# Attention followed by expert routing on one core: expert work set between attention steps, domain ids loaded in runs, transposes set between output tiles

## The chip, the cores and the metric

The kernel runs on one core of a Trainium2 chip. The metric is device time in microseconds (us); what is compared is the median of several executions. Engines: TensorE (PE; PEld is its weight load), VectorE (DVE), ScalarE (ACT), GpSimd (POOL) and SyncE (SP). DMAs are issued from SP, ACT and POOL, each in the order of its own instruction stream.

## What is computed

```python
q_pool = q.reshape(B, H, S // 2, 2, D).mean(axis=3)      # B = 8, H = 8, S = 1152, D = 64
scores = scale * np.matmul(q_pool, k.transpose(0, 1, 3, 2))
attn = np.exp(scores - max) / sum
x = np.matmul(attn, v)                                   # as (B * 576, 512): 4608 tokens
for e in range(8):
    mask = domain_id == e
    out[mask] = np.maximum(x[mask] @ w1[e], 0.0) @ w2[e] # 512 -> 1024 -> 512
```

Queries are pooled in pairs, attention runs over all 1152 keys, and each of the 4608 tokens then goes through the one expert that its domain id names. The ids do not depend on the attention.

## The kernel before

**Attention.** The 64 heads are taken as 32 pairs, four pairs to a batch. A pair is 12 steps, 384 steps `t` in all (`p`, `s_` are the pair and the step in it). In a step TensorE makes the scores of 432 query-key columns for both heads (`score`, L410; two PSUM buffers `s`), ScalarE takes the exponential of them in one instruction (`expo`, L425), and in nine of twelve steps TensorE also multiplies one earlier block of exponentials with the values (`av`, L435: ten matmuls of 65 columns). The table `AVS` (L477) says in which steps: all but 2, 6 and 10 of a pair, the last two falling into the next pair. `evac` (L449) divides by the sums and writes the pair's part of `xb`, the batch's rows, with VectorE. Loads run ahead by two or three pairs: queries on SyncE (`load_q`, three buffers), keys and values on POOL (`load_k`, `load_v`, three buffers each). `prep_q`, `prep_k`, `prep_v` cast and sort them on VectorE, and `burst_k`, `burst_q` transpose them on TensorE in steps 2 and 6 for the next pair, by one of two PSUM buffers `tp`.

**Routing.** `rt_a` to `rt_d` and `rt_tok` work out on VectorE, with two small matmuls (L199, L204), to which row of the DRAM tensor `x_slot` each token goes: 640 slots an expert, of which the first 256 are kept for tokens of the first four batches (`KO`, `IB`), and an overflow area. The ids come by nine small copies on ScalarE's queue (L158). `init_x` fills the 640-slot areas with a pattern in four copies on SyncE; it depends on `pat` alone. After the last pair of a batch, `put_x` scatters its rows to `x_slot` from POOL (`scatter`, L338). Weights of experts 0 to 4 are loaded by POOL from step 60 on.

**Experts.** After the attention the pools of the attention are released, and `run` (L621) takes one expert at a time: `get_x` loads its slots, `turn` transposes them (per tile of 128 slots four matmuls and one copy by VectorE or ScalarE), `stage1` and `stage2` are the two matrix products, and each tile of output rows is scattered to `out` by POOL. Experts 0 to 2 run in two parts, first their 256 early slots, then the other 384; experts 3 to 7 run with all 640 at once.

**What sets the order.** Each engine executes in the order in which the program is written (`manual_schedule`); what waits for what is worked out by a tracker of tiles and of whole DRAM tensors. Two writes into `x_slot`, or a read and a write, wait for each other in program order, except scatters among themselves, which are declared free of each other (group `xscat`).

## Time and profile before

| | us |
|---|---|
| runs | 538.62, 539.15, 542.89; median 539.15 |
| the profiled execution | 537.33 |
| its span, first to last instruction | 535.5 |
| PE, ACT, DVE, POOL busy in it | 462.0, 351.0, 220.3, 163.5 |
| mean granted TensorE clock | 0.948 |

The page of the profile gives busy times, the span in 40 slices, the DMA queues, the chain of work that ended last, and groups of instructions by line. Its other views list instructions in order of time (start, length, engine, line, what is written <- what is read, how many, and in brackets the idle time before and what ended it), the waits summed by who waited for whom, stretches of time with each engine's busy time, and DMA issues with their median time to landing. A busy TensorE is not TensorE at its peak, since the ends of matmuls are modelled; their starts are not.

### The profile page before, as it was taken

Reading aid. Unit: us, or ns where it says so; the run is one execution under the profiler, and the core shown is the slowest. Engines: PE = TensorE matmul, PEld = TensorE weight load, DVE = VectorE, ACT = ScalarE, POOL = GpSimd, SP = SyncE. Lnnn points to the kernel's source line nnn. Section 1 sums busy time; section 2 is a strip of 40 time slices with the busy share of each in tenths; the row PEclk is TensorE's granted clock in tenths of the full one; section 3 lists DMA queues with packets and bytes.
Section 4 is the critical chain, followed back from the end, with each engine's and each line's share of the span. In section 5 each row is a group of like instructions: output and inputs, shape, how many; then the busy total and the mean of one; then the engine's idle time right before and its main releaser. Section 6 shows DMA issues by size and latency. Waiting matters only on the chain.

```text
span 535.5 us, 12899 instructions
## 1 busy us (share of the span) xinstructions
PE 462.0 (86%) x5536; PEld 323.6 (60%) x5536; DVE 220.3 (41%) x515; ACT 351.0 (66%) x470; POOL 163.5 (31%) x278
## 2 busy tenths in 40 slices
PE   6038999999999999999999999539899999999990
PEld 3026777777777777777777777425544555455440
DVE  4038545455554555545455553102332223223220
ACT  1117999999999999999999999512222323223310
POOL 5001108207225145154173040111335521321321
PEclk9558999999999999999999999959999999999996
DMA  9969846988999949959969930022329994221211
GB/s 227 224 125 241 199 92 143 245 171 173 237 184 193 215 106 223 190 114 231 215 127 236 195 69 2 15 91 69 109 78 220 238 248 149 96 95 44 85 61 37
DMA packets 57172, 80.48 MB, mean 150 GB/s; under 512 B 8590, under 2 KB 43150, under 8 KB 57104
## 3 DMA queue, kind: packets, MB, share of 16 engines
q0 software_dynamic: 34928, 49.54, 47.4%
q1 hardware_dynamic: 17424, 29.99, 19.9%
q10 hardware_dynamic: 4752, 0.02, 0.8%
q8 instruction: 45, 0.74, 0.6%
q14 instruction: 23, 0.19, 0.1%
HBM read 95.46 MB, written 20.49 MB: 217 GB/s over the span
## 4 chain that ended last, share of the span: by engine, by line
ACT 47%; issue 26%; DMA 11%; POOL 8%; DVE 2%; PE 2%; POOLq 0%; ACTq 0%; SPq 0%; DVEq 0%
ACT e L431 47%; POOL out_dram L341 6%; DMA w2h<-in_moe_w_dram 5%; DMA dom<-in_moe_domain_id_dram 3%; DMA x_slot<-pat 2%; PE s L419 1%; POOL x_slot L341 1%; PE acc L442 1%; POOL gap L339 1%; DMA xs<-x_slot 1%; DMA x_slot<-xb,addr 0%; DVE xb L459 0%; DVE sc L212 0%; POOLq L341 0%; POOL vs L96 0%
## 5 line engine op out<-in xcount | busy, mean ns | idle before, releaser
L431 ACT ACTIVATE e<-s 128x864 f16<-128x864 f32 x384 | 302.1, 899 | 38.2 <-DMA dom<-in_moe_domain_id_dram 23.1
L419 PE MATMUL s<-qz,kq 128*128 128x432 f16 (+2 forms) x1152 | 205.9, 287 | 23.4 <-ACT e L431 22.4
L442 PEld LDWEIGHTS <-e 128*128 128x128 f16 x2880 | 127.8, 98 | 41.7 <-DVE xb L459 2.8
L442 PE MATMUL acc<-v,e 128*128 128x65 f16 x2880 | 136.6, 194 | 2.4 <-DVE xb L459 2.1
L419 PEld LDWEIGHTS <-kq 128*128 128x128 f16 x1152 | 102.2, 97 | 49.7 <-issue 30.3
L341 POOL DMA_INDIRECT x_slot<-xb,addr x40 | 43.5, 1087 | 130.0 <-issue 130.0
L591 PE MATMUL hp<-xt,w1h 128*128 128x128 f16 (+3 forms) x512 | 75.9, 301 | 5.0 <-DVE xt L579 3.2
L341 POOL DMA_INDIRECT out_dram<-osb,xs x40 | 39.6, 990 | 121.3 <-ACT osb L613 101.9
L607 PE MATMUL op<-w2h,hT 128*128 128x512 f16 x320 | 70.9, 379 | 0.0
L591 PEld LDWEIGHTS <-w1h 128*128 128x128 f16 x512 | 43.8, 98 | 36.6 <-issue 8.1
L596 ACT ACTIVATE hT<-hp 128x640 f16<-128x640 f32 (+2 forms) x44 | 24.6, 559 | 51.1 <-PE hp L591 48.8
L613 ACT COPY osb<-op 128x512 f32<-128x512 f32 x24 | 14.1, 586 | 60.0 <-PE op L607 60.0
L457 DVE RECIPROCAL rr<-acc 128x5 f32<-128x5 f32 x64 | 12.2, 190 | 100.0 <-PE acc L442 100.0
L607 PEld LDWEIGHTS <-hT 128*128 128x128 f16 x320 | 31.1, 98 | 35.6
L598 DVE TENSOR_SCALAR hT<-hp 128x640 f16<-128x640 f32 (+2 forms) x44 | 28.3, 643 | 55.0 <-PE hp L591 53.8
L96 POOL DMA_DIRECT2D vs<-in_v_dram x32 | 23.8, 743 | 79.5 <-DVE v L366 77.7
L459 DVE TENSOR_TENSOR xb<-acc,rr 128x320 f16<-128x320 f32 x64 | 31.5, 492 | 2.8 <-DVE rr L457 0.4
L357 DVE TENSOR_TENSOR qp<-q 96x768 f16<-96x768 f32 x32 | 30.2, 945 | 1.5 <-DMA q<-in_q_dram 1.5
L615 DVE COPY osb<-op 128x512 f32<-128x512 f32 x16 | 11.1, 692 | 45.5 <-PE op L607 45.5
L404 DVE COPY qz<-tp 64x576 f16<-64x576 f16 x64 | 28.7, 449 | 1.0
L575 PE MATMUL xp<-ident,xs 128*128 128x128 f16 x160 | 14.0, 223 | 16.7 <-DMA xs<-x_slot 13.1
L375 DVE COPY kp<-k 128x576 f16<-128x576 f16 x62 | 25.0, 445 | 2.6 <-DMA k<-in_k_dram 2.6
(80 smaller groups left out, 232.3 us busy)
## 6 DMA issues: line engine op xcount, KB each, us to landing
q<-in_q_dram SPq DMA_DIRECT2D x32, 576.0 KB, 7.4
vs<-in_v_dram POOLq DMA_DIRECT2D x32, 288.0 KB, 10.1
k<-in_k_dram POOLq DMA_DIRECT2D x31, 288.0 KB, 10.6
w1h<-in_moe_w_dram POOLq DMA_DIRECT2D x16, 512.0 KB, 8.4
w2h<-in_moe_w_dram POOLq DMA_DIRECT2D x16, 512.0 KB, 14.8
x_slot<-pat SPq DMA_DIRECT2D x4, 1285.0 KB, 11.6
xs<-x_slot SPq DMA_DIRECT2D x5, 642.5 KB, 9.5
xs<-x_slot SPq DMA_DIRECT2D x3, 385.5 KB, 3.1
```

Of the source, the lines that this page charges most:

```text
L341: ins = nc.gpsimd.indirect_dma_start(out=dst[:, :], out_offset=bass.IndirectOffsetOnAxis(ap=ap, axis=0), in_=src, in_offset=None, **kw,)
L357: nc.vector.tensor_tensor(out=qp[:, :, :, :].rearrange("p j h d -> p h j d"), in0=q2[:, :, :, 0:D], in1=q2[:, :, :, D : 2 * D], op=ALU.add,)
L375: nc.vector.tensor_copy(kp[:, :, hh, :], loaded[p]["k16"][:, hh, :, :])
L404: nc.vector.tensor_copy(qz[p % 2][r][lo : lo + 64, :], mt[lo : lo + 64, P : P + Sp])
L419: nc.tensor.matmul(s[:, r, o : o + n], lhsT=kq[p][:, c * P : (c + 1) * P], rhs=qz[p % 2][r][:, q0 : q0 + n], start=True, stop=True,)
L431: nc.scalar.activation(e_[:, :, o : o + W], st.pop(t)[:, :, 0:W], AF.Exp, bias=0.0, scale=0.0625)
L442: nc.tensor.matmul(acc[p][h][:, i * (D + 1) : (i + 1) * (D + 1)], lhsT=e_[:, h, o + QO[i] : o + QO[i] + P], rhs=v16[p % NV][:, c, h, 0 : D ...
L459: nc.vector.tensor_tensor(out=xb[b][:, :, hh * D : (hh + 1) * D], in0=a[:, :, 0:D], in1=rr[:, :].unsqueeze(2).broadcast_to([P, NQ, D]), op ...
L591: nc.tensor.matmul(hp_[:, lo : lo + n], lhsT=w1h[:, cc, f * P : (f + 1) * P], rhs=xt[:, cc, lo : lo + n], start=cc == 0, stop=cc == ND - 1,)
L596: nc.scalar.activation(hT[:, f, 0:m], hp_[:, 0:m], AF.Relu)
L598: nc.vector.tensor_scalar(out=hT[:, f, 0:m], in0=hp_[:, 0:m], scalar1=0.0, scalar2=None, op0=ALU.max)
L607: nc.tensor.matmul(op_[:, :], lhsT=hT[:, f, i * P : (i + 1) * P], rhs=w2h[:, f, :], start=f == 0, stop=f == NF - 1,)
```

## The change

Five things are changed together.

1. The ids are loaded by one copy on SyncE as they lie, 96 partitions with 12 words in a run for each of eight batches, and VectorE copies them to their places in steps 14 to 19 (`rt_dom`). Query pair 1 is loaded from ScalarE's queue, which also casts half of the first keys. The first value and key loads of POOL stand behind its set-up.
2. Routing runs in steps 14 to 33 instead of up to step 15, `init_x` in steps 34, 37, 40 and 43 instead of 20 to 29. In steps 36 to 43, eight new scatters, one per expert, write pattern rows behind each expert's overflow rows; the list of overflowed tokens that was made at the end goes away (`g_over`; this branch runs only when an expert has over 640 tokens).
3. Experts 0 to 3 have their first 256 slots computed in the attention's steps. Each is cut into 17 units: one of transposes, eight of the first product, eight of the second. From step 220 on one unit stands at the end of steps 0, 4, 7 and 10 of a pair. They share one PSUM buffer (`mpsum`), for which `tpsum` goes from two to one. What is left when the steps end runs straight behind them.
4. Behind the attention come one part of 256 slots (expert 4), five of 384 (experts 0 to 4) and three of 640 (5 to 7). Loads are issued two parts ahead, and the transposes of the next part stand between the output tiles of the present one.
5. The ids' copy into `xb` by POOL stands after the last pair of a batch instead of before the first.

**SyncE, from the third load to query pair 6.** Before (`q_232`, `q_439`, `q_646`, `q_843`, `q_1038` are query pairs 2 to 6; brackets name the semaphores waited for, DMASW of POOL's DMAs, DMAHW of the other queues'):

```order
L87 DMA q_232<-in_q_dram 96x2x768
L87 DMA q_439<-in_q_dram 96x2x768 [waits DMAHW6_49,DMAHW2_49,DVE_49]
L166 DMA x_slot<-pat 128x10x514 [waits DMAHW7_49,Pool_49]
L166 DMA x_slot<-pat 128x10x514 [waits DMAHW0_49]
L87 DMA q_646<-in_q_dram 96x2x768 [waits DMAHW3_49,DMAHW1_49,DVE_49]
L166 DMA x_slot<-pat 128x10x514 [waits DMAHW2_49]
L166 DMA x_slot<-pat 128x10x514 [waits DMAHW3_49]
L87 DMA q_843<-in_q_dram 96x2x768 [waits DMAHW4_49,DVE_49]
L644 TENSOR_LOAD ovi [waits DVE_49]
```

Now (`q_211` to `q_858` are pairs 2 to 5, `q_1072` is pair 6):

```order
L119 DMA dom<-in_moe_domain_id_dram 96x8x12
L88 DMA q_211<-in_q_dram 96x2x768
L88 DMA q_387<-in_q_dram 96x2x768 [waits DMAHW2_49,DVE_49]
L88 DMA q_623<-in_q_dram 96x2x768 [waits DMAHW3_49,DVE_49]
L165 DMA x_slot<-pat 128x10x514 [waits DMAHW0_49,Pool_49]
L88 DMA q_858<-in_q_dram 96x2x768 [waits DMAHW5_49,DMAHW1_49,DVE_49]
L741 TENSOR_LOAD ovi [waits DVE_49]
L741 ISA x2
L165 DMA x_slot<-pat 128x10x514 [waits DMASW3_49]
L165 DMA x_slot<-pat 128x10x514 [waits DMASW7_49,DMASW6_49,DMASW4_49]
L165 DMA x_slot<-pat 128x10x514 [waits DMASW3_49,DMAHW4_49,DMASW1_49,DMASW0_49]
L88 DMA q_1072<-in_q_dram 96x2x768 [waits DMAHW6_49,DVE_49]
```

The last three initialising copies now wait for DMAs of POOL (the scatters between them in the program), and query pair 6 stands behind all four instead of query pair 5.

**POOL, steps 40 to 50 of the change** (`vs` is value pair 6, `k_1112` key pair 7; DMAHW3 and DMAHW4 are the third and fourth initialising copy):

```order
L349 DMA x_slot<-pat,padr 41984x514 [waits DMAHW3_49,DMASW0_49]
L347 MEMSET gap 1x1 [waits Pool_49]
L349 DMA x_slot<-pat,padr 41984x514 [waits DMASW1_49]
L97 DMA vs<-in_v_dram 128x2x576 [waits DMASW2_49,DVE_49]
L347 MEMSET gap 1x1 [waits Pool_49]
L349 DMA x_slot<-pat,padr 41984x514 [waits DMASW3_49]
L347 MEMSET gap 1x1 [waits Pool_49]
L349 DMA x_slot<-pat,padr 41984x514 [waits DMAHW4_49,DMASW4_49]
L471 COPY xb<-tok 128x5 [waits DVE_49]
L105 DMA k_1112<-in_k_dram 128x2x576 [waits DMASW5_49,DVE_49]
```

Before, only loads stood here ahead of the first `put_x`; now scatters that wait for the initialising copies stand ahead of these loads.

**TensorE, the end of a step with a unit** (`acc` is a value product, `m` a unit of the second product, `s` the next step's scores):

```order
L450 LDWEIGHTS e
L450 MATMUL acc_4382<-v_0_97,e 128x65
L547 LDWEIGHTS h_4023
L547 MATMUL m<-w2h,h_4023 128x512
L547 LDWEIGHTS h_4023
L547 MATMUL m<-w2h,h_4023 128x512
L427 LDWEIGHTS kq
L427 MATMUL s<-qz_0_93,kq 128x432
```

Before, the scores of the next step stood right behind the value products.

The diff, cut to what the steps above speak of:

```diff
+    mpsum = att.enter_context(tc.tile_pool(name="mpsum", bufs=1, space=bass.MemoryType.PSUM))
-    tpsum = att.enter_context(tc.tile_pool(name="tpsum", bufs=2, space=bass.MemoryType.PSUM))
+    tpsum = att.enter_context(tc.tile_pool(name="tpsum", bufs=1, space=bass.MemoryType.PSUM))
...
     load_q(0)
-    load_v(0)
-    load_k(1)
-    load_v(1)
-    load_q(1)
+    dom = perm.tile([QP, B, NJ, 2], I32, name="dom")
+    nc.sync.dma_start(
+        dom[:, :, :, :].rearrange("p b j t -> p b (j t)"),
+        moe_domain_id.bitcast(I32).rearrange("(b p j t) -> p b (j t)", b=B, p=QP, j=NJ),
+    )
...
-    for i in range(NQ):
-        m, end = 0, 64 if i == 0 else P
-        while m < end:
-            j, pp = divmod(QO[i] + m, QP)
-            n = min(QP - pp, end - m)
-            nc.scalar.dma_start(dom[m : m + n, :, i : i + 1], dv_[pp : pp + n, :, j, 0:1])
-            m += n
...
+    load_v(0)
+    load_k(1)
+    load_v(1)
...
+    def rt_dom(j):
+        if j == 0:
+            nc.vector.memset(dal[64:P, :, 0:1], -1.0)
+        for a in range(QP // 32):
+            x = j * QP + 32 * a
+            i, m = (0, x) if x < 64 else (1 + (x - 64) // P, (x - 64) % P)
+            nc.vector.tensor_copy(dal[m : m + 32, :, i], dom[32 * a : 32 * a + 32, :, j, 0])
...
+        nc.vector.tensor_tensor(out=padr[:, :], in0=ov[:, :], in1=padb[:, :], op=ALU.add)
...
+    load_q(1, nc.scalar)
...
+    def add_expert(e):
+        h0 = {}
+
+        def u_load():
+            h0["xs"] = get_x(fill, e, 0, NA)
+
+        def u_turn():
+            mt = mpsum.tile([P, NA, ND, P], F16, name="m")
+            for i in range(NA):
+                for cc in range(ND):
+                    nc.tensor.transpose(
+                        mt[:, i, cc, :], in_=h0["xs"][:, i, cc * P : (cc + 1) * P],
+                        identity=ident16[:, :],
+                    )
+            h0["xt"] = fill.tile([P, ND, NA * P], F16, name="xt0")
+            nc.vector.tensor_copy(
+                h0["xt"][:, :, :].rearrange("p c (i n) -> p i c n", i=NA), mt[:, :, :, :]
+            )
+
+        def u_up(f):
+            if f == 0:
+                h0["h"] = fill.tile([P, NF, NA * P], F16, name="h0")
+            mt = mpsum.tile([P, 512], FP32, name="m")
+            for cc in range(ND):
+                nc.tensor.matmul(
+                    mt[:, 0 : NA * P], lhsT=wts[e][0][:, cc, f * P : (f + 1) * P],
+                    rhs=h0["xt"][:, cc, :], start=cc == 0, stop=cc == ND - 1,
+                )
+            nc.vector.tensor_scalar(
+                out=h0["h"][:, f, :], in0=mt[:, 0 : NA * P], scalar1=0.0, scalar2=None, op0=ALU.max
+            )
+
+        def u_down(i, g):
+            if g == 0:
+                h0["o"] = mpsum.tile([P, 512], FP32, name="m")
+            for f in (2 * g, 2 * g + 1):
+                nc.tensor.matmul(
+                    h0["o"][:, :], lhsT=h0["h"][:, f, i * P : (i + 1) * P], rhs=wts[e][1][:, f, :],
+                    start=f == 0, stop=f == NF - 1,
+                )
+            if 2 * g + 2 == NF:
+                osb = fill.tile([P, Dm], FP32, name="osb0")
+                nc.vector.tensor_copy(osb[:, :], h0["o"][:, :])
+                scatter(out, osb[:, :], h0["xs"][:, i, Dm:XW].bitcast(I32), "oscat", N - 1)
...
-        if t in (20, 23, 26, 29):
-            init_x((t - 20) // 3)
+        if t in (34, 37, 40, 43):
+            init_x((t - 34) // 3)
+        if 36 <= t < 36 + E:
+            scatter(x_dram, pat[:, :], padr[:, t - 36 : t - 35], "xscat")
...
+        if t == 212:
+            for e in range(FE):
+                add_expert(e)
+            loads.pop(0)()
+        if t >= 220 and main and s_ in FS and units:
+            units.pop(0)()
...
+    while units:
+        units.pop(0)()
     att.close()
...
             scatter(out, osb[:, :], ids(i), "oscat", N - 1)
+            for _ in range(2 if len(between) > n - 1 - i else 1):
+                if between:
+                    between.pop(0)()
...
+    runs = [(e, 0, NA) for e in range(FE, 5)]
+    runs += [(e, NA, NTC) for e in range(5)] + [(e, 0, NTC) for e in range(5, E)]
+    xs = {r: get_x(xsb, *r) for r in runs[:2]}
```

More of the change, by code (lines that the diff above doesn't have):

```diff
@@ L267, in rt_d @@
     def rt_d():
-        slot, dall = rt["slot"], rt["dall"]
+        slot = rt["slot"]
         isov = perm.tile([P, NT], FP32, name="isov")
@@ L279, in rt_d @@
         nc.vector.scalar_tensor_tensor(
-            out=ext[:, :], in0=dall[:, :], scalar=float(CAP), in1=ext[:, :], op0=ALU.mult, op1=ALU.add
+            out=ext[:, :], in0=dall, scalar=float(CAP), in1=ext[:, :], op0=ALU.mult, op1=ALU.add
         )
@@ L601, in stage1, with stage2 @@
         return hT
-    def stage2(w2h, hT, n, ids):
+    def stage2(w2h, hT, n, ids, between=()):
+        between = list(between)
         for i in range(n):
```

201 lines of the change are left out of this document (92 added, 109 removed).

## The prediction

> **What bounds the kernel now.** I read the page first, for its slices and its chain of waits.
>
> ```profile
> span 535.5 us, 12899 instructions
> ACT  1117999999999999999999999512222323223310
> ACT 47%; issue 26%; DMA 11%; POOL 8%; DVE 2%; PE 2%; POOLq 0%; ACTq 0%; SPq 0%; DVEq 0%
> ```
>
> A slice is 13.4 us. ScalarE is full in slices 5 to 25 only; ahead of that it hardly works for some 45 us, and behind it TensorE does the experts alone. So there are three stages with three limits, and the change touches each. The list of waits says what holds the first one up, and the timeline of the first 45 us says when:
>
> ```profile
> ACT e L431 <- DMA dom<-in_moe_domain_id_dram: 23.1, 1, 23.1
> ACT e L431 <- PE s L419: 14.8, 9, 10.2
> DVE dall L182 <- DMA x_slot<-pat: 20.0, 1, 20.0
> ```
>
> ```profile
> 5.58 19.76 ACTq L158 DMA_DIRECT2D dom<-in_moe_domain_id_dram  x9
> 11.11 1.62 PE L419 MATMUL s<-qz,kq 128*128 128x432 f16 x6 [0.67 <-DVE qz L404]
> 14.68 0.81 DVE L375 COPY kp<-k 128x576 f16<-128x576 f16 x2 [2.65 <-DMA k<-in_k_dram]
> 25.38 1.67 ACT L431 ACTIVATE e<-s 128x864 f16<-128x864 f32 x2 [23.13 <-DMA dom<-in_moe_domain_id_dram]
> 39.87 0.89 ACT L431 ACTIVATE e<-s 128x864 f16<-128x864 f32 x1 [10.16 <-PE s L419]
> ```
>
> Scores stand ready from 11.1, but ScalarE's own queue issues nine copies of the domain ids until 25.34, and its first exponential stands behind them. Then VectorE waits 20.0 for the last of those ids, TensorE's count matmul (L199) waits for VectorE, and the scores stand behind that matmul until 39.87. From step 20 on ScalarE is the limit. The chain shows nothing but exponentials from there; the timeline has the last 36 without a break, 28.30 us or 0.786 a step:
>
> ```profile
> 56.74 3.08 ACT e L431 x4
> 314.20 28.30 ACT L431 ACTIVATE e<-s 128x864 f16<-128x864 f32 x36 [0.17 <-ACT e L431]
> ```
>
> The last 36 of 384 steps begin with step 348; 314.20 less 56.74 is 328 steps of 0.785, so 56.74 is step 20, and step 67 begins at 56.74 + 47 x 0.785 = 93.6.
>
> **Part 1, the start.** The nine copies leave ScalarE's queue; ids come in runs of 12 words behind query pair 0 on SyncE. Nothing asks for them until step 14. What is late next is key pair 1: its load is near the head of POOL's queue (used at 14.68, above), and now stands behind POOL's set-up, of which the filling of `pat` is the last:
>
> ```profile
> 2.17 0.78 POOL L104 DMA_DIRECT2D k<-in_k_dram  x1
> 5.54 0.47 POOL pat L161
> ```
>
> With a value load ahead of it, it goes out near 6.9 instead of 2.17 and loses 4.7 us of lead, but what it shares the engines with at first is less. Bounds for its landing: 14 (no later than now) to 19 (the whole delay); I take 15, nearer the first, since pairs 0 to 2 of queries and pair 0 of values now land ahead of or beside it instead of nine id copies. Its cast (0.8), eight transposes, and a score later, step 3 starts at 17.0 and step 20 at 30.3.
>
> **Part 2, routing and initialisation.** VectorE's routing moves from steps 3 to 15 to steps 14 to 33. Today it loads VectorE so:
>
> ```profile
> 42.00:56.00 14.00, 11.82 (x161) 9.12 (x160) 11.40 (x36) 10.74 (x15) 1.43 (x2) 0.87 1.09 249
> ```
>
> The third number is VectorE: 11.4 busy of 14. From 39.87 (step 4) to 56.74 (step 20) 16 steps took 16.9 instead of 12.5, so 4.4 us were lost to a late VectorE. I charge the same again (bounds 2, if the spread over more steps helps, and 6, since 18 short copies of ids are new): step 66 starts at 30.3 + 46 x 0.785 + 4.4 = 70.8.
>
> The larger matter is an order of writes. `x_slot` is one tensor to the dependency tracker. The initialising copies (steps 34, 37, 40, 43) now stand between the new pad scatters (steps 36 to 43), so each waits for the landing of the other: copy 0, pad 0, copy 1, pads 1 to 3, copy 2, pads 4 to 6, copy 3, pad 7. SyncE holds query pair 6 behind copy 3; POOL holds key pair 7 behind pad 7. Today the four copies go out in twos and no scatter stands between.
>
> ```profile
> 22.54 2.42 SPq L166 DMA_DIRECT2D x_slot<-pat  x2
> 24.57 11.07 DMA x_slot<-pat
> x_slot<-pat SPq DMA_DIRECT2D x4, 1285.0 KB, 11.6
> x_slot<-xb,addr POOLq DMA_INDIRECT x40, 4.2
> 346.23 0.97 POOL x_slot L341
> 347.51 0.97 POOL x_slot L341
> ```
>
> Two copies took from 22.54 to 35.64, 6.6 each with queries in front of them; the median to landing is 11.6. Alone, as in the new chain, I take 7.5. A scatter is issued every 1.28 and lands in 4.2 (median); with idle queues I take 3. The first pad waits for `padr`, made at the end of the routing of step 28: step 28 starts at 30.3 + 6.3 + 1.5 = 38, and about 5 us of VectorE work stand there, so 43. Then pad 0 lands +3.2, copy 1 +7.5, three pads with a key load between, 3.4 to issue and 3 to land, +6.4, copy 2 +7.5, three more +6.4, copy 3 and query pair 6 behind it +10: 41 us, so query pair 6 lands at 84. VectorE prepares it at step 63, and TensorE's transposes of it, at the end of step 66 (71.2), stand in the one queue with all later scores. It is prepared at 85, so about 14 us are lost, and step 67 starts at 86. With 11.6 a copy it would be 98, with 6.6 it would be 83. Against 93.6 now, the start gains **7.6**, not the 22 that it has gained by step 66. Key pair 7 (issued near 83) and the next loads have lost their lead while the first weights come: I add **1** of further waits.
>
> The Trainium skill ("DMA: Bandwidth & Descriptors", section "Anatomy of one DMA — SWDGE (gpsimd) path") fits a DMA at about 2.0 us and its bytes over 436 GB/s; for a copy of 1285 KB that would be an estimated 5.0, and the whole kernel 7.5 shorter. The rows above, 6.6 at the least, speak against it.
>
> **Part 3, units between the steps.** 55 of the 68 units fall into steps 220 to 383 (3 in pair 18, 4 in each of pairs 19 to 31). How much room has TensorE in a step? Behind a stall, where it waits for nobody:
>
> ```profile
> 51.80 0.53 PE L419 MATMUL s<-qz,kq 128*128 128x432 f16 x2
> 52.17 0.46 PE L442 MATMUL acc<-v,e 128*128 128x65 f16 x10
> 52.47 0.70 PE L419 MATMUL s<-qz,kq 128*128 128x144 f16 x4
> ```
>
> By the starts, scores take 0.37 and ten value matmuls 0.30: 0.67 of 0.785, so 0.11 is free in a step with values, and 0.41 in one without. The busy digits of the page (9) hide this, since a matmul's end is modelled. A down unit is two matmuls of 512 columns, 0.44 by the 40 in 8.80 below; an up unit is four of 256, the same columns. Of the slots 0, 4, 7 and 10 only 10 has no value step. Two score buffers give no lead: a score starts when the exponential two steps back ends, so the excess delays ScalarE. 41 units x (0.44 - 0.11) = 13.5, 14 units x 0.03 = 0.4; I take **12**, a little less, for latencies that overlap. Bounds: 0, if the buffers cushion it all, and 55 x 0.44 = 24, if none of the room can be used. VectorE copies each unit out, 0.43 to 0.7, which goes into its idle half:
>
> ```profile
> 200.00:300.00 100.00, 97.23 (x1508) 77.01 (x1505) 52.31 (x126) 99.85 (x129) 39.05 (x61) 1.00 0.96 192
> L598 DVE TENSOR_SCALAR hT<-hp 128x256 f16<-128x256 f32 x12 | 5.1, 425 | 11.2 <-PE hp L591 9.9 <-ACT hT L596 1.3
> 342.56 0.45 PE L442 MATMUL acc<-v,e 128*128 128x65 f16 x9 [0.33 <-ACT e L431]
> ```
>
> The Trainium skill ("TensorE: Matmul & The Clock Gate", section "Back-to-back issue gap") gives about 131 ns for a 512-column matmul in a stream; a down unit would be an estimated 0.26 and this part some 4 us less. The row of 40 matmuls says 220 ns, and I go by it.
>
> The 13 units left over run behind the last step, five ups and two output tiles, each a matmul group and VectorE's copy: 5 x 1.1 + 2 x 2.7 = 11. They are hidden: from TensorE's last value matmuls (342.56 above) to the first expert matmul (357.84) lie 15 us of scatters and loads. Without that cover they would cost their 11.
>
> **Part 4, the tail.** Stage starts today, for 256, 384 and 640 slots:
>
> ```profile
> 357.84 5.21 PE L591 MATMUL hp<-xt,w1h 128*128 128x256 f16 x32 [0.67 <-ACT xt L581]
> 367.77 4.37 PE L591 MATMUL hp<-xt,w1h 128*128 128x256 f16 x32 [0.82 <-DVE xt L579]
> 371.97 3.62 PE L607 MATMUL op<-w2h,hT 128*128 128x512 f16 x16
> 386.81 5.90 PE L591 MATMUL hp<-xt,w1h 128*128 128x384 f16 x32 [0.52 <-DVE xt L579]
> 392.55 5.34 PE L607 MATMUL op<-w2h,hT 128*128 128x512 f16 x24
> 397.73 0.61 PE L575 MATMUL xp<-ident,xs 128*128 128x128 f16 x8
> 399.58 5.91 PE L591 MATMUL hp<-xt,w1h 128*128 128x384 f16 x32 [0.52 <-DVE xt L579]
> 484.92 8.85 PE L591 MATMUL hp<-xt,w1h 128*128 128x512 f16 x64 [0.21 <-ACT xt L581]
> 493.61 8.80 PE L607 MATMUL op<-w2h,hT 128*128 128x512 f16 x40
> 504.64 8.85 PE L591 MATMUL hp<-xt,w1h 128*128 128x512 f16 x64 [0.21 <-ACT xt L581]
> 513.33 8.80 PE L607 MATMUL op<-w2h,hT 128*128 128x512 f16 x40
> ```
>
> From 357.84 to 522.1 the tail is 164.3. Transposes between output tiles leave only their matmuls, 0.25 a tile, on TensorE; their copies run under the next output tile, except where a run's last transpose stands behind its last output tile (0.7). Run of 256: 4.2 + 3.6 + 0.7 + 0.7 = 9.2. Of 384: 5.74 + 5.18 + 0.75 = 11.7 (now 12.8). Of 640: 8.7 + 8.65 + 1.25 = 18.6 (now 19.7, from 484.92 to 504.64). After the change there is one of 256, five of 384 and three of 640 in place of three, three and five: 9.2 + 4 x 11.7 + 12.9 (more transposes, exposed end) + 2 x 18.6 + 17.4 = 123.5. It saves **41** (bounds 36, if the copies stall TensorE, and 43).
>
> **The sum.** 535.5 - 7.6 + 1 + 12 - 41 = 499.9 of span. The profiled execution took 537.33, 1.8 more than its span, and lies 1.8 under the median of the runs (539.15) and 1.3 under the lowest (538.62). So 501.7 for a profiled execution; I say **502** for the median, since most of that spread is noise.
>
> **The rivals.** (a) The loads keep their lead: the chain of copies and pads ends before step 63, by quick landings or an earlier `padr`. For it: slices with little traffic near 36 us. Against: seven landings in a row. 502 - 14 = 488. (b) The units hide: ScalarE never waits. For it: TensorE's free 0.11 to 0.41 a step. Against: no lead beyond two buffers. 502 - 12 = 490. (c) The queues never refill after the chain: keys, values and the first weights share one queue, and pairs 7 to 10 wait 4 us each for them. 502 + 16 = 518; about the same if a unit costs its full 0.44. (d) On the other side: the one PSUM buffer of the units makes TensorE wait at each unit for VectorE's copy of the unit before. One round trip is 0.44 + 0.2 + 0.43 and a wait in VectorE's order, some 1.3; 55 x 1.3 = 72 in place of 12 gives 562. It turns slower from 0.9 a unit on. Against: units are three steps, 2.3 us, apart.
>
> **Chances.** Forecast 0.48 (own range 494 to 510), (a) 0.16, (b) 0.13, (c) 0.18, (d) 0.05. A measurement of this kernel can tell about 1% from no change. The range 481 to 521 takes in (a), (b) and (c) with the bounds of their costs and leaves out (d) and the far ends. Faster by over 1%: 0.94; within 1%: 0.01; slower: 0.05.
>
> **What would show it.** The first exponentials before 13; a wait of TensorE or VectorE for a query or key load near 71 to 85; copies of `x_slot` on SyncE some 14 apart; ScalarE steps from 220 on at 9.4 + 0.9 a pair; experts of 640 slots every 18.6. It is wrong if ScalarE shows no gap near step 66, if its steps from 220 on keep 0.785, or if the tail from the first 256-slot run is not near 123.

## The result, and the profile after

The changed kernel takes **525.64 us** (median of 4 runs, 523.70 to 526.27) where the kernel before takes 538.92 (539.15 stood above; a fourth run of it took 538.69): a ratio of **0.973**, 95% interval 0.968 to 0.978. It is faster, by 13 us and not by the 37 that were forecast, and lies 4.6 above the end of the range. The profiled execution took 525.88, its span is 524.1.

The page of the changed kernel, in the same order as that of before (span, ScalarE by slices of 13.1 us, chain of waits by engine, group of the exponentials):

```profile
span 524.1 us, 12917 instructions
ACT  2579890499999999949999899999412323323220
PE 31%; issue 23%; DMA 18%; ACT 14%; POOL 9%; DVE 2%; POOLq 0%; SPq 0%; ACTq 0%
L439 ACT ACTIVATE e<-s 128x864 f16<-128x864 f32 x384 | 308.4, 895 | 59.7 <-PE s L427 56.5
```

ScalarE begins early, but slices 7 and 8 hold a hole (0 and 4), and slice 18 a smaller one (4), that were not there before. ScalarE is 14% of the chain where it was 47%, TensorE 31% and DMA 18%. The 384 exponentials wait 59.7 us in all. The timeline shows where the largest piece lies; a row gives start, length, engine, line, what is written <- read, count, and in brackets the idle time before and what ended it:

```profile
19.95 0.89 ACT L439 ACTIVATE e<-s 128x864 f16<-128x864 f32 x1 [5.50 <-PE s L427]
79.13 0.89 ACT L439 ACTIVATE e<-s 128x864 f16<-128x864 f32 x1 [0.42 <-PE s L427]
98.10 0.89 ACT L439 ACTIVATE e<-s 128x864 f16<-128x864 f32 x1 [18.08 <-PE s L427]
...
95.67 0.95 DVE L365 TENSOR_TENSOR qp<-q 96x768 f16<-96x768 f32 x1 [18.95 <-DMA q<-in_q_dram]
96.68 0.66 PE L404 MATMUL tp<-ident,qp 96*128 96x96 f16 x6 [18.12 <-DVE qp L365]
```

The first three rows are steps 3, 66 and 67. Between the last two ScalarE waits 18 us, TensorE the same for VectorE, and VectorE 18.95 for query pair 6: the chain of the prediction, at its place. The chain of waits, read from 37 to 96 us (start, length, what; its shorter rows between these are left out), gives the links of it:

```profile
37.55 12.99 issue
50.55 3.10 DMA x_slot<-pat,padr
53.66 6.77 DMA x_slot<-pat
61.22 1.00 POOL x_slot L349
64.61 4.74 DMA x_slot<-pat,padr
69.43 6.87 DMA x_slot<-pat
77.07 0.31 POOL x_slot L349
80.39 4.28 DMA x_slot<-pat,padr
85.28 10.36 DMA q<-in_q_dram
```

In the tail, parts of 384 slots stand 11.58 apart and parts of 640 stand 18.45 apart:

```profile
410.05 5.90 PE L678 MATMUL hp<-xt,w1h 128*128 128x384 f16 x32
421.63 5.90 PE L678 MATMUL hp<-xt,w1h 128*128 128x384 f16 x32
475.67 8.86 PE L678 MATMUL hp<-xt,w1h 128*128 128x512 f16 x64
494.12 8.86 PE L678 MATMUL hp<-xt,w1h 128*128 128x512 f16 x64
```

Cut at the starts of four exponentials, the span compares with the forecast so (the forecast's 86, its 213.4 - 7.6 + 1, its 128.2 + 12, and 194 - 41):

| stretch | before | forecast | measured |
|---|---|---|---|
| start to step 67 | 93.5 | 86.0 | 98.1 |
| step 67 to 220 | 119.9 | 120.8 | 124.7 |
| step 220 to 383 | 128.2 | 140.2 | 149.6 |
| step 383 to the end | 194.0 | 153.0 | 151.8 |
| span | 535.5 | 500.0 | 524.1 |

So the tail came as forecast, and three stretches ahead of it came 12, 4 and 9 us too long. The runs below ask why. Where two kernels ran on different chips, their ratios to the kernel before on the same chip are compared: it took 540.2 on one and 533.1 and 533.2 on the two others. On the first ran the pads behind the copies, the later first unit, all units behind and half of each unit; on the second the kernel without pads, the halves, the tail and the early loads; on the third the rest. A ratio is followed by its interval; a single run has none.

### The profile page after: what moved, and what is told of

Its sections match the earlier page's. It is cut to its first block, busy times and chain, and to the rows that moved or that the text cites. A ratio compares the mean times of both kernels' runs of the same rounds, so it can differ in the third digit from the quotient of the medians.

```text
span 524.1 us, 12917 instructions
## 1 busy us (share of the span) xinstructions
PE 453.3 (86%) x5536; PEld 321.4 (61%) x5536; DVE 234.3 (45%) x561; ACT 348.1 (66%) x455; POOL 172.2 (33%) x294
## 4 chain that ended last, share of the span: by engine, by line
PE 31%; issue 23%; DMA 18%; ACT 14%; POOL 9%; DVE 2%; POOLq 0%; SPq 0%; ACTq 0%
PE s L427 16%; ACT e L439 14%; PE acc L450 8%; POOL out_dram L349 5%; DMA x_slot<-pat 3%; DMA out_dram<-osb,xs 3%; DMA k<-in_k_dram 3%; DMA w2h<-in_moe_w_dram 2%; DMA x_slot<-pat,padr 2%; POOL x_slot L349 2%; PE m L535 2%; DMA xs<-x_slot 2%; DMA q<-in_q_dram 2%; PE m L547 2%; PE tp L391 1%
## 5 line engine op out<-in xcount | busy, mean ns | idle before, releaser
L439 ACT ACTIVATE e<-s 128x864 f16<-128x864 f32 x384 | 308.4, 895 | 59.7 <-PE s L427 56.5
L427 PE MATMUL s<-qz,kq 128*128 128x432 f16 (+2 forms) x1152 | 208.3, 290 | 12.1 <-ACT e L439 7.1
L450 PE MATMUL acc<-v,e 128*128 128x65 f16 x2880 | 139.1, 195 | 1.6 <-DVE xb L466 0.8
L678 PE MATMUL hp<-xt,w1h 128*128 128x384 f16 (+3 forms) x384 | 61.4, 311 | 1.8 <-DVE xt L664 0.9
L695 PE MATMUL op<-w2h,hT 128*128 128x512 f16 x256 | 59.8, 379 | 0.0
L678 PEld LDWEIGHTS <-w1h 128*128 128x128 f16 x384 | 34.1, 99 | 28.9 <-issue 4.6
L97 POOL DMA_DIRECT2D vs<-in_v_dram x32 | 24.2, 757 | 65.0 <-DVE v L374 52.9
L685 DVE TENSOR_SCALAR hT<-hp 128x384 f16<-128x384 f32 (+2 forms) x36 | 22.8, 632 | 49.1 <-PE hp L678 40.1
L701 ACT COPY osb<-op 128x512 f32<-128x512 f32 x20 | 11.7, 586 | 49.5 <-PE op L695 40.3
L683 ACT ACTIVATE hT<-hp 128x384 f16<-128x384 f32 (+2 forms) x36 | 19.8, 550 | 36.0 <-PE hp L678 35.6
L464 DVE RECIPROCAL rr<-acc 128x5 f32<-128x5 f32 x64 | 12.2, 190 | 70.4 <-PE acc L450 61.1
L695 PEld LDWEIGHTS <-hT 128*128 128x128 f16 x256 | 24.1, 98 | 24.3
L466 DVE TENSOR_TENSOR xb<-acc,rr 128x320 f16<-128x320 f32 x64 | 31.5, 492 | 2.6
L404 PE MATMUL tp<-ident,qp 96*128 96x96 f16 x192 | 14.0, 210 | 18.1 <-DVE qp L365 18.1
L391 PE MATMUL tp<-ident,kp 128*128 128x128 f16 x256 | 20.0, 222 | 6.9 <-DVE kp L383 6.4
## 6 DMA issues: line engine op xcount, KB each, us to landing
w1h<-in_moe_w_dram POOLq DMA_DIRECT2D x16, 512.0 KB
w2h<-in_moe_w_dram POOLq DMA_DIRECT2D x16, 512.0 KB
```

The source lines that it names most:

```text
L97: nc.gpsimd.dma_start(vs[:, :, :, :], v[b, h : h + 2].rearrange("h (p c) d -> p h c d", p=P))
L391: nc.tensor.transpose(mt[:, c * P : (c + 1) * P], in_=kp[:, c, :, :].rearrange("p h d -> p (h d)"), identity=ident16[:, :],)
L427: nc.tensor.matmul(s[:, r, o : o + n], lhsT=kq[p][:, c * P : (c + 1) * P], rhs=qz[p % 2][r][:, q0 : q0 + n], start=True, stop=True,)
L439: nc.scalar.activation(e_[:, :, o : o + W], st.pop(t)[:, :, 0:W], AF.Exp, bias=0.0, scale=0.0625)
L450: nc.tensor.matmul(acc[p][h][:, i * (D + 1) : (i + 1) * (D + 1)], lhsT=e_[:, h, o + QO[i] : o + QO[i] + P], rhs=v16[p % NV][:, c, h, 0 : D ...
L466: nc.vector.tensor_tensor(out=xb[b][:, :, hh * D : (hh + 1) * D], in0=a[:, :, 0:D], in1=rr[:, :].unsqueeze(2).broadcast_to([P, NQ, D]), op ...
```

## Experiments: the hole at step 67

**Pads behind the copies.** The theory is the prediction's own: copies and pad scatters alternate, and each waits for the other.

```diff
-        if 36 <= t < 36 + E:
-            scatter(x_dram, pat[:, :], padr[:, t - 36 : t - 35], "xscat")
+        if 44 <= t < 44 + E:
+            scatter(x_dram, pat[:, :], padr[:, t - 44 : t - 43], "xscat")
```

> The eight pad scatters stand in steps 44 to 51 instead of 36 to 43, so that all four initialising copies stand ahead of them; nothing else differs from the changed kernel. Theory (the alternation of copies and pads is what keeps query pair 6 back): the copies go out in twos behind the query loads, query pair 6 is issued well before 60 us and the gap of 18.97 us in ScalarE's steps at step 67 closes to 0 to 3. Step 67 starts near 80 instead of 98.1, and the kernel takes 525.6 - 16 to - 19 = 507 to 510. Rival 1 (the DMA queues are simply full of loads and 5 MB of copies by then, whatever the order): query pair 6 lands late all the same, the gap stays over 8 and the time over 517. Rival 2 (the pads wait for padr, and the key and value loads behind them on POOL are late next): a new gap for a key or value load at steps 60 to 90, time 515 to 520.

Measured: 512.03, ratio 0.9455 (0.9406 to 0.9503). The gap at step 67 is gone, but step 67 starts at 89.18 and not at 80, for new gaps had opened at steps 44 to 57:

```profile
65.30 0.89 ACT L439 ACTIVATE e<-s 128x864 f16<-128x864 f32 x1 [2.72 <-remote]
68.96 1.67 ACT L439 ACTIVATE e<-s 128x864 f16<-128x864 f32 x2 [2.77 <-PE acc L450]
```

The rows are steps 45 and 46. Their scores were ready (the score matmuls of step 46, which stand behind those of step 45, began at 62.63), and no key, value or query was missing. So rival 2, a late load, was not it either. The pads themselves, eight scatters from 59.6 to 70.4, were suspected, and left out:

```diff
-        if 36 <= t < 36 + E:
-            scatter(x_dram, pat[:, :], padr[:, t - 36 : t - 35], "xscat")
```

> The eight pad scatters are left out: the pattern rows behind each expert's overflow rows are not written (no token of these inputs uses them). Copies stay at steps 34 to 43. With the pads in steps 44 to 51 the copies went out without waiting for pads, yet 5.7 us were lost at steps 44 to 46, where ScalarE stood still with its scores ready, and some 5 more up to step 57; the time was 512.0. Theory (the burst of eight scatters beside landing copies causes these new stalls): step 67 starts near 80 instead of 89.2, time 502 to 506. Rival (the 5 MB of copies, landing by 59.5 at the latest, cause them by themselves): step 67 stays at 87 to 90, time 510 to 513. If the alternation of copies and pads were not the cause of the first loss at all, the gap of 18 at step 67 would come back: 525.

Measured: 498.17, ratio 0.9322 (0.9277 to 0.9368); step 67 at 80.35. Step 67 is where the theory had it, but this run was on a chip where the kernel before takes 533.1 and not 540.2. The version with the pads behind the copies therefore ran a second time, on the third chip:

> The version with the pads in steps 44 to 51 once more, because the chip on which it ran (the kernel before at 540.2 there) and the one of the run without pads (533.1 there) differ. Theory (the burst of pads itself stops ScalarE for 5.7 us at steps 44 to 46 and slows the steps to 57): the stalls are there again whatever the chip, step 67 starts 8 to 9 later than without pads (80.35), at 88 to 90, ratio to the kernel before near 0.9455. Rival (the stalls belong to that chip, not to the pads): no stall at 44 to 46, step 67 near 81, ratio near 0.932 to 0.934.

Measured: 498.09, ratio 0.9352 (0.9299 to 0.9404), step 67 at 79.88, with the pads in place. SyncE, ScalarE:

```profile
32.94 6.69 SPq L165 DMA_DIRECT2D x_slot<-pat  x3
46.50 50.75 SPq L88 DMA_DIRECT2D q<-in_q_dram  x6
...
59.08 0.89 ACT L439 ACTIVATE e<-s 128x864 f16<-128x864 f32 x1 [0.32 <-PE s L427]
60.32 50.24 ACT L439 ACTIVATE e<-s 128x864 f16<-128x864 f32 x64 [0.35 <-PE s L427]
```

The last three copies go out within 6.7 us where they took 31.5 before, query loads follow at 46.5, and from 60.32 on 64 exponentials run without a break. The rival held: the stalls of 2.7 do not come from the pads as such, and the theory of the burst falls. The gap of 18 to 20 us is the alternation's: a kernel that keeps it (the one of the section on the tail) lost 20.2 at step 67 on the chip on which the kernel without pads lost nothing there.

## Experiments: the units between the steps

**A later first unit.** In the changed kernel the first unit finds no data:

```profile
227.59 1.03 PE L521 MATMUL m<-ident,xs 128*128 128x128 f16 x8 [4.59 <-DMA xs<-x_slot]
229.38 0.89 ACT L439 ACTIVATE e<-s 128x864 f16<-128x864 f32 x1 [5.70 <-PE s L427]
```

The load of `xs` waits for the scatters of batch 3. POOL issued the last of them at 211.71, SyncE issued the load at 220.03, and it landed 7.51 later. All scores stand behind these transposes.

```diff
-        if t >= 220 and main and s_ in FS and units:
+        if t >= 232 and main and s_ in FS and units:
```

> The first unit stands at step 232 instead of 220; the first expert's slots are still asked for at step 212. Theory (the first unit stands on TensorE's queue before its slots have landed, because the load waits for the last scatters of batch 3): the wait of 4.59 us at the first transposes and the slow steps behind it, about 8 us in all, go away. Four more units are left behind the last step, 1.1 to 1.5 each, of which 2.4 is covered by TensorE's wait for the first slots of the tail: some 2 to 3 come back. Time 525.6 - 5 to - 6 = 520. Rival (the units' own cost makes up all of the 21 us between step 220 and the end, the wait only takes the place of it): no more than 1 to 2 us, 523 to 525.

Measured: 526.38, ratio 0.9741 (0.9692 to 0.9789): no gain. Yet steps 220 to 383 took 142.6 and not 149.6: 7 of the 8 that the theory had. Of these 5.7 came back behind the last step, with 157.5 from its exponential to the end and not 151.8, and 1.7 were lost ahead of step 220, which this run reached later. The leftover units show how the 5.7 came about:

```profile
370.39 0.68 PE L535 MATMUL m<-xt,w1h 128*128 128x256 f16 x4 [1.44 <-DVE xt L526]
371.59 1.01 PE L535 MATMUL m<-xt,w1h 128*128 128x256 f16 x4 [0.52 <-DVE h L539]
373.12 1.01 PE L535 MATMUL m<-xt,w1h 128*128 128x256 f16 x4 [0.51 <-issue]
```

```profile
372.00:385.00 13.00, 9.39 (x35) 4.57 (x34) 2.97 (x7) 0.00 (x0) 3.96 (x8) 0.52 0.50 157
```

The last row is a stretch of the windows view of the same kernel: its length, then busy time and instructions of PE, PEld, DVE, ACT and POOL, then the granted clock, 0.52, DMA share and GB/s. An up unit takes 1.53 there and not the 1.11 that it took in the changed kernel, whose leftovers ran at 1.00. So the time lies nearer the rival's 523 to 525, but for a reason that neither theory had.

**All units behind the last step.**

```diff
-        if t >= 220 and main and s_ in FS and units:
+        if t >= NST and main and s_ in FS and units:
```

> No unit stands in a step; all 68 run behind the last step. Theory (the 21.4 us that steps 220 to 383 take longer than before are the units and the first unit's wait, nothing else): these steps go back to 128 to 130 us. The 68 units run by themselves at 1.11 an up unit and 2.67 a set of four downs, about 16.3 an expert, 65 in all, of which the last exponential's cover takes some 15: first expert of the tail near 418 instead of 388, time 525.6 + 30 = 556. Rival (the single buffer tp or the later start slows these steps with or without units): steps 220 to 383 stay at 140 or more and the time is 567 or more.

Measured: 578.83 (one run). Steps 220 to 383 take 130.4, so the units and the first unit's wait do account for the stretch. But the 68 units took 82 us (from 356.82 to 439.19) and not 65, at half the clock for long stretches:

```profile
363.00:378.00 15.00, 11.64 (x35) 4.62 (x34) 2.82 (x6) 0.00 (x0) 2.90 (x6) 0.50 0.19 62
```

The Trainium skill ("TensorE: Matmul & The Clock Gate", section "A second HAM failure mode: psum-queue depth-cycling") tells of a kernel whose TensorE idles briefly and often between groups of matmuls, as it goes round its PSUM buffers, so that its clock swings between half and full. This run, with one buffer and 0.52 idle before most units, swings too: 0.50 in the row above and from 403 to 419, 1.00 from 378.4 to 381.7 and from 395.5 to 402.2. The changed kernel's own 13 leftovers, with the same 0.52 before most of them, kept 1.00 for their ten us, so how often and how long it must idle the runs leave open.

**Half of each unit's matmuls.** Two matmuls in place of four, one in place of two; that part of the contraction is left out.

```diff
-            for cc in range(ND):
+            for cc in range(ND // 2):
...
-            for f in (2 * g, 2 * g + 1):
+            for f in (2 * g,):
...
```

> Each up unit has two matmuls instead of four and each down unit one instead of two: half of the contraction of the early slots of experts 0 to 3 is left out, the copies by VectorE, the buffers and the places stay. Theory (a unit costs what its matmuls, 0.44, exceed the room in a step with values, 0.11): 0.22 less a unit at steps 0, 4 and 7 of a pair, so a pair falls from about 10.45 to 9.7 us, and 41 such units give 9 us; the first unit's wait stays. Time 516 to 517. Rival (what costs is latency, the wait for the one buffer m and VectorE's copy in its order): the pair stays above 10.2 and the time within 2 of 525.6.

Measured: 521.21 (one run). By the starts of exponentials twelve steps apart (median over steps 244 to 371), a pair takes 9.65; in the changed kernel 10.24, before 9.40. So the size of the matmuls sets the cost, as the theory had it (9.7), and not a fixed latency. The changed kernel's rows show one pair of 10.2, 304.36 to 314.58, with nine exponentials between the rows shown; the half units' row has 39 steps in 31.19, 0.80 a step or 9.6 a pair:

```profile
304.36 2.46 ACT L439 ACTIVATE e<-s 128x864 f16<-128x864 f32 x3 [0.15 <-PE s L427]
...
314.58 2.46 ACT L439 ACTIVATE e<-s 128x864 f16<-128x864 f32 x3
```

```profile
299.45 31.19 ACT L439 ACTIVATE e<-s 128x864 f16<-128x864 f32 x39
```

A step with a whole unit takes 1.05 at places 0 and 4, 1.11 at 7 and 0.77 at 10; with half a unit 0.83, 0.83 and 0.89. The time fell by less than expected because this run was already 3.6 us later at step 220.

**Halves at nine places.** If a half unit costs 0.045 a step, all the work fits in as halves. Each unit is cut in two, its transposes and up matmuls likewise (left out of this diff).

```diff
-    FS = (0, 4, 7, 10)
+    FS = (0, 3, 4, 5, 7, 8, 9, 10, 11)
...
-            for f in (2 * g, 2 * g + 1):
+            for f in (g,):
...
+            if s_ == 10 and units:
+                units.pop(0)()
```

> Each unit is cut in two halves (one tile of transposes; two matmuls of 256 columns; one of 512) and the halves stand in the eight value steps 0, 3, 4, 5, 7, 8, 9, 11 of a pair, one each, and two in step 10: ten halves a pair instead of four whole units. Same work in all, from step 220. Theory (a step with values has room of some 0.11 to 0.18, a half unit is 0.22): by the run with half of each unit's matmuls, which lost 0.045 at steps 0 and 4 and 0.10 at 7, a pair takes 9.43 + 0.4 to 0.5 = 9.9 instead of 10.45, although it holds five whole units instead of four; 13.6 pairs give 7, and nothing is left over behind the last step (that part was hidden already). The first unit's wait stays. Time 518 to 519. Rival (each place where TensorE changes to the unit's buffer costs a wait of its own, for VectorE's copy): nine places cost 0.15 or more each, the pair takes 10.8 or more, time 528 or more.

Measured: 535.34, ratio 1.001 (0.998 to 1.005): the rival's time. A pair takes 11.54. Steps 4 and 10 show where most of it goes:

```profile
239.14 0.94 DVE L365 TENSOR_TENSOR qp<-q 96x768 f16<-96x768 f32 x1
240.01 0.41 DVE L546 TENSOR_SCALAR h<-m 128x256 f16<-128x256 f32 x1
240.47 0.38 PE L540 MATMUL m<-xt,w1h 128*128 128x256 f16 x2 [0.57 <-DVE h L546]
241.26 0.89 ACT L439 ACTIVATE e<-s 128x864 f16<-128x864 f32 x1 [0.68 <-PE s L427]
...
256.60 0.69 DVE L560 COPY osb<-m 128x512 f32<-128x512 f32 x1 [0.98 <-PE m L554]
257.35 0.38 PE L554 MATMUL m<-w2h,h 128*128 128x512 f16 x1 [0.78 <-DVE osb L560]
```

Step 4 takes 1.57 and step 10, which holds two halves, 1.48. In step 10 a unit begins in the step in which the last one ended, and where it needs the one buffer anew its first matmul waits 0.51 to 0.78 for VectorE to empty it. In step 4 the last unit ended a step earlier, but VectorE's copy of it stands behind the cast of queries (the first row), and the matmul waits 0.57 to 0.85. A unit that begins in step 9, one step after the last one ended, waits 0.11 at most, so to be neighbours is not enough. At the other value steps a half costs 0.03 to 0.14, near what was expected, and 0.20 in step 3. That is the prediction's rival (d), brought about by the edit: in the changed kernel no unit from step 222 on waits for the buffer; here the wait is decisive, where VectorE's copy has no time or other work ahead of it.

**No units at all**, on the version with the early loads (below), whose ratio is 0.9204:

```diff
-    FE = 4
+    FE = 0
```

> On the version with the early loads and the later routing (ratio 0.9204): no expert work between the steps at all; the experts 0 to 4 run their first 256 slots in the tail, each as one part. Theory: steps 220 to 383 fall back from 144.4 to 129 to 130 (15 less), the tail gets four parts of 256 longer, 9.3 to 10.2 each, 38 to 40: net 23 to 25 us slower, ratio 0.963 to 0.967. Rival (what the units take from the steps is nearly what they save in the tail): within 8 us, ratio below 0.936.

Measured: 509.07, ratio 0.9567 (0.9512 to 0.9621). Steps 220 to 383 take 127.7 in place of 144.4, the tail 185.6 in place of 150.5. Moving four parts of 256 slots into the steps saves 35 and costs 16.7, of which 5.0 is the first unit's wait (steps 220 to 232 took 15.3, and 9.4 + 0.84 would do). So the theory held and not its rival, but its size was off: the units are worth 18 in span and not 23 to 25, since the parts cost less than its 38 to 40 and the steps gave back more than its 15.

## Experiment: the tail

```diff
-            for _ in range(2 if len(between) > n - 1 - i else 1):
-                if between:
-                    between.pop(0)()
+        for fn in between:
+            fn()
```

> The transposes of the next part stand behind the last output tile of the present one instead of between the tiles; loads are still asked for two parts ahead. Theory (of the 41 us that the tail got shorter, the place of the transposes is the smaller part, the three times 256 slots that moved out the larger): each of eight transitions between parts costs 1.1 to 1.2 us more, 384 slots take 12.8 instead of 11.6, 640 take 19.7 instead of 18.45, in all 9 us: time 534 to 535. Rival (the loads two parts ahead are what makes the tail quick, the place of the transposes does little): 526 to 529.

Measured: 529.53 where the kernel before takes 533.1 (one run, 0.993). This kernel keeps the alternation, and its gap at step 67 was 20.2. Parts of 384 now stand 12.78 apart, parts of 640 19.77:

```profile
405.41 5.91 PE L678 MATMUL hp<-xt,w1h 128*128 128x384 f16 x32 [0.52 <-DVE xt L664]
418.19 5.91 PE L678 MATMUL hp<-xt,w1h 128*128 128x384 f16 x32 [0.52 <-DVE xt L664]
457.11 8.90 PE L678 MATMUL hp<-xt,w1h 128*128 128x512 f16 x64 [0.19 <-ACT xt L666]
476.88 3.31 PE L678 MATMUL hp<-xt,w1h 128*128 128x512 f16 x22 [0.21 <-ACT xt L666]
```

From the last exponential to the end it takes 160.5 and not 151.8: the place of the transposes is worth 8.7 of the 42 by which the tail fell, near the 9 of the theory. The time came out 5 below its 534 all the same, near the rival's 526 to 529, because this run had reached step 383 at 367.2 and the changed kernel's own at 372.4. Four moved parts of 256 slots cost 35 in the run without units, so they are the rest of the 42, and little is left for the loads issued two parts ahead, which no run tries by themselves.

## Experiments: the start, and a faster version

**Early loads and later routing matmuls**, with the pads behind the copies:

```diff
+    load_v(0)
+    load_k(1)
+    load_v(1)
+
     warm = perm.tile([P, 288], F16, name="warm")
...
-        if t == 21:
-            rt_b()
+        if t == 23:
+            rt_b()
+        if t == 24:
+            rt_b2()
...
```

> On the version with the pads in steps 44 to 51 (512.0): POOL's first three loads are issued ahead of its set-up as before the change, and the two routing matmuls stand in steps 23 and 24 instead of both in 21, the routing behind them up to three steps later. Theory: key pair 1 lands near 14 instead of 17.3, so step 3 starts near 17 instead of 20.4; VectorE is through with the one-hot rows when TensorE comes to the first matmul and the other does not wait for the copy of its buffer, so of the 3.55 lost at step 22 some 2.5 go away; step 44 comes 5 us sooner and the time is 506 to 507. Rival (what follows is set by the landing of copies and loads at 55 to 75 us, not by ScalarE's steps): the gain is lost again by step 67, which stays at 88 to 89, time 511 to 512.

Measured: 491.37, ratio 0.9204 (0.9155 to 0.9253), 1.6% under the 0.9352 of the pads behind the copies alone. Key pair 1 is cast at 13.13, 17.29 in the changed kernel, step 3 starts at 16.72, step 67 at 74.08 and not at 79.88: the gain of the start is kept. What is left of VectorE's lateness shows at step 39:

```profile
48.59 0.20 DVE L323 TENSOR_TENSOR tok<-jj,bof 128x40 int32<-128x40 f32 x1
48.70 0.80 DVE L388 COPY kp<-k 128x576 f16<-128x576 f16 x2
49.56 0.62 PE L396 MATMUL tp<-ident,kp 128*128 128x128 f16 x8 [3.15 <-DVE kp L388]
50.59 0.89 ACT L444 ACTIVATE e<-s 128x864 f16<-128x864 f32 x1 [3.19 <-PE s L432]
```

The cast of the next keys stands behind a row of short routing instructions, TensorE's transposes wait 3.15 for it, and the scores behind them.

**Units from step 224**, then that **and the routing spread**:

```diff
-        if t >= 220 and main and s_ in FS and units:
+        if t >= 224 and main and s_ in FS and units:
```

> On the version with the early loads and the later routing (ratio 0.9204): units from step 224 on, so that the first stands in step 226, six steps or 4.7 us later than in 220. Theory: the loss of 5.6 at steps 220 to 224 shrinks to below 1; two more units are left behind the last step, 1.1 to 1.5 each, about 2.4 of which TensorE would have waited for the tail's first slots anyway, so next to nothing comes back: ratio 0.910 to 0.912. Rival (as with 232, where all 7 came back): the tail behind the last exponential grows by 4 or more, ratio 0.918 or more.

```diff
-        if t == 32:
+        if t == 42:
             rt_d()
-        if t == 33:
+        if t == 45:
             rt_tok()
```

> As with units from step 224, and besides the end of the routing is spread: the addresses in step 42, the token numbers in step 45 instead of 32 and 33. Theory (the 3.31 lost at step 39 are VectorE's row of short routing instructions ahead of the cast of key pair 4, for which TensorE's transposes and all later scores wait): 2.3 to 3 of it go away and do not come back at step 46, where VectorE has no cast to make: ratio 0.904 to 0.907, the best version. Rival (the loss moves to the next cast or to the scatters, which wait for the addresses): within 1 us of the version with units from 224.

Measured: 488.47, ratio 0.9154 (0.9097 to 0.9212), and 483.90, ratio 0.9084 (0.9032 to 0.9135). The first takes 5.4 less in steps 220 to 383 (138.9), and gave 3.8 back behind them, its leftovers once more at half the clock from 339 us on (1.01 for an up unit's matmuls, which take 0.60 at the full one); its interval overlaps that of the version before it, so a gain in time is not shown by it alone. The second takes 138.9 as well, its leftovers at full clock, and 151.1 behind the last exponential. Step 39 loses 0.97 in place of 3.31, and 47 exponentials run without a break from 48.86; then the key load of pair 8 is late:

```profile
48.86 36.92 ACT L444 ACTIVATE e<-s 128x864 f16<-128x864 f32 x47 [0.26 <-PE s L432]
85.76 0.81 DVE L388 COPY kp<-k 128x576 f16<-128x576 f16 x2 [5.29 <-DMA k<-in_k_dram]
87.77 0.89 ACT L444 ACTIVATE e<-s 128x864 f16<-128x864 f32 x1 [1.98 <-PE s L432]
```

At step 67 it is 5.0 ahead of the version with units from 224, at step 220 only 1.7: with ScalarE no longer held up, the loads are the next limit. Of the 4.9 of span between the two profiles the spread routing thus keeps 1.7; the other 3.3 lie behind the last exponential, where the leftovers happened to keep the full clock, which nothing in this edit aimed at. That part is luck. It is the fastest version here, 9.2% under the kernel before; 0.904 to 0.907 was expected, which the interval holds.

## Why the prediction was wrong, step by step

Three terms failed: the time lost to a late VectorE, the chain of writes by its size, and the first unit's wait for its data, which was put at nothing. The rows show VectorE late at steps 21 and 39 of the changed kernel:

```profile
37.34 0.30 PE L207 MATMUL tp<-oh,one 128*128 128x320 f16 x1 [2.35 <-DVE oh L192]
38.41 0.30 PE L212 MATMUL tp<-oh,lst 128*128 128x320 f16 x1 [0.77 <-DVE sc L208]
39.16 1.67 ACT L439 ACTIVATE e<-s 128x864 f16<-128x864 f32 x2 [3.50 <-PE s L427]
...
54.90 0.62 PE L391 MATMUL tp<-ident,kp 128*128 128x128 f16 x8 [1.79 <-DVE kp L383]
```

- **What bounds the kernel:** right. ScalarE in the steps, TensorE in the tail.
- **Part 1, key pair 1 at 15:** mis-sized. It was cast at 17.29, inside the bounds of 14 to 19 but nearer the far one, and step 3 started 3 us late. With the loads ahead of POOL's set-up it starts at 16.7.
- **Part 2, 4.4 lost to a late VectorE (bounds 2 to 6):** this step failed. From step 3 to 66 are 63 steps, 49.5 at full speed; 59.2 passed, so 9.7 were lost. Two mechanisms were missing. At step 21 TensorE's two routing matmuls waited for VectorE's one-hot rows and then for the copy out of the one `tp` buffer (3.6), and at step 39 the cast of keys stood behind short routing instructions (1.9). The other gaps come to about the 4.4 forecast. The runs bear both out: with the two matmuls in steps of their own 1.0 and 0.95 were lost in place of 3.6, and with the routing spread step 39 lost 0.97. The diff showed `tpsum` cut to one buffer, but the prediction set no price on it.
- **Part 2, the chain of writes:** right in mechanism and place, mis-sized. `padr` came near 50 and not at 43, mostly the lateness above. From the first pad to the landing of query pair 6 it took 45.1 and not 41: the copies were quicker than the 7.5 assumed (6.8 and 6.9), the two legs of three pads slower (8.9 and 8.4 for 6.4, with landings of 4.7 and 4.3 for 3), the last copy and the query load 11 and not 10. With `padr` 7 and the chain 4 late, step 67 was at 98 and not at 86, and the start lost 4.6 where it was to gain 7.6. The estimate of 5.0 from the Trainium skill ("DMA: Bandwidth & Descriptors", section "Anatomy of one DMA — SWDGE (gpsimd) path") was further off than the rows' 6.6; that section fits DMAs of GpSimd, and these copies go out from SyncE.
- **The 1 of further waits:** 4.8 in the changed kernel (124.7 between steps 67 and 220), 2.7 to 5.3 in the four runs on the chip at 540. On the two others it was 1.4 in the two kernels that keep the alternation, all of it right behind the gap, and none in five that do not (119.87, as before the change). So some 1.4 is the chain's (1 was forecast); the rest are stalls that only the changed kernel's own run and those on the chip at 540 show (the last section), and loads did not keep running late, rival (c). Only the fastest version, ahead of its loads, loses 3.4 to a late one.
- **Part 3, 12 for the units:** right for the units, wrong for the stretch, which took 21.4 more than before. A pair costs 0.84 more (0.9 forecast), 11.4 in all. That the first unit would wait for its own slots was not foreseen, a term put at nothing: steps 220 to 232 took 17.6 in place of 10.2, which is 7.4. Some 2.6 more are stalls of 0.4 to 1.4 at steps 297, 345, 346 and 375, which the kernel of the section on the tail, with the same steps on the chip at 533.1, does not show. The load was asked for at step 212, but the scatters that it waits for had been issued only at 211.7 us, behind weights and loads on POOL's queue.
- **The 13 leftovers, hidden, 11 if they were not:** right (373.6 to 384.4, the tail's first slots came at 386.8).
- **Part 4, 41:** right, 42. The rows of 9.2, 11.7 and 18.6 came as 10.2, 11.6 and 18.45.
- **The range** rested on bounds for each cost by itself. The lateness of VectorE, of `padr` and of the chain add up since each waits for the one ahead, and the range held one of them at its far end, not three.

By the sum, 24.2 of span are missing: 12.1 up to step 67 (8.3 of it by step 66), 3.9 up to step 220, 9.4 in the steps with units (7.4 the first unit's wait), and the tail gave 1.2 back.

## What to carry to other kernels

Where a tracker sees a DRAM tensor as one piece, set all writes of one queue ahead of those of another: alternating them turns transfers that would overlap into a chain of landings, and whatever stands behind it on those queues pays. When work is set into another engine's slack, price three things apart: the slack by the start times, the first item's data (what must have landed, behind which queue), and the distance between items that share a buffer. And when one term of a sum sets the start of the next, their errors add; the range has to carry them together.

## What the hardware showed that was not expected

- **Chips differ.** The kernel before took 540.2 on one chip and 533.1 and 533.2 on two others. On the first, ScalarE stood still for 2.7 us at a time beside POOL's scatters with its scores ready; the same kernel on the third showed none of it (512.0 against 498.1). TensorE stood still with it (3.08 before the scores at 66.25). The changed kernel's own profile has shorter stalls of this kind beside the scatters of later batches; on the second chip the kernel of the section on the tail, the same up to step 383, has none and is there 5.2 sooner. What holds the engines was not settled.
- **The clock of stop-and-go units.** Leftover units with 0.52 us of idle before most of them kept a granted clock of 1.00 in the changed kernel and in the fastest version, and fell to 0.50 or 0.52 in others. The version with the pads behind the copies did both, in its two runs on two chips (its last eight matmuls in 1.89 and in 3.57). What decides was not settled; it is worth some 3 to 6 us with 15 to 17 units, and some 17 with 68, against the 65 that was expected of them.
- **The room in a step.** In steps 0 and 4 a unit of 0.44 made the step 0.26 longer, half a unit of 0.22 made it 0.04 longer: either way 0.18 is free there, and not the 0.11 read from the starts of the matmuls. In step 7, where a unit costs 0.30 and half a unit 0.09, it is 0.14 and 0.13.
